# A recurrent attention and a snake MLP in one kernel: v of 13 tiles loaded as float by SyncE, and Strassen's products for two more groups of tiles

## The chip, the cores and the metric

The kernel runs on one core of one Trainium2 chip. A core has five engines, each with its own list of instructions that it takes in order: TensorE (PE in the profile, with its weight loads as PEld), VectorE (DVE), ScalarE (ACT), GpSimd (POOL) and SyncE (SP), which here issues DMAs only. GpSimd issues DMAs too. Instructions of different engines wait for each other by semaphores. The metric is the device time of one execution in microseconds (us), the median over several runs.

## The reference

Per batch and head a decaying state is summed up over 768 tokens, and each token's q reads it. What comes out is an input of an MLP with the function h + sin(alpha h)^2 / alpha. All arrays are float32.

```python
B, H, S, D = 4, 8, 768, 64            # q, k, v: [B, H, S, D]
gamma = 1.0 - 2.0 ** (-5.0 - np.arange(H))
for t in range(S):
    state = gamma[None, :, None, None] * state + np.einsum('bhd,bhe->bhde', k[:, :, t], v[:, :, t])
    y[:, :, t] = np.einsum('bhd,bhde->bhe', q[:, :, t], state) / np.sqrt(D)
x = y.transpose(0, 2, 1, 3).reshape(B * S, H * D)      # [3072, 512]
h = x @ w_in                                           # w_in [512, 2048]
s = np.sin(alpha * h)
out = (h + s * s / (alpha + 1e-09)) @ w_out            # w_out [2048, 512]
```

## The kernel before

The 3072 tokens are 24 tiles of 128 (six per batch). `order`, also called `P`, is the order in which tiles are worked on: P0 to P3 are the first tiles of the four batches, then come the rest of batches 0 and 1 (P4 to P13), and from P14 on batches 2 and 3, in the end alternating. Ten groups follow: g0 with four tiles, g1 to g8 with two each, g9 with four.

**Attention.** A tile's scores, their mask, and the product with v are computed as blocks; what earlier tiles left is read from a state (s_f in float, s_q in bf16). v is scaled by a decay factor (`scale_v`, line 185) before it is used. `burst` (line 458) works on one tile and starts the next one's scores; `pair` (line 537), used for P16 to P21, does two tiles of different batches at once, with one PSUM tile y of two banks. Both write TensorE instructions that need the scaled v of their tiles. q and k are transposed by a DMA that SyncE issues (`turn`, line 294, tile qkT, six buffers) or, for early tiles, by TensorE.

**Loads.** GpSimd issues loads that change float to bf16. For the 11 tiles P0 to P10 a load brings one tile (`load_chunk`); for the 13 others, called wide, `load_seq` (line 131) brings all wide tiles of a batch, with eight DMAs (four heads by two halves of the partitions) for each of q, k and v, into qk_seq and v_seq. Batch 1 has three wide tiles, batches 2 and 3 five each. `scale_v` then works in place, for P9 to P14 on VectorE, for others on GpSimd.

**MLP.** A phase g from 1 to 9 (`phase`, line 878) computes the hidden layer of group g in slots, and beside it the output layer of group g-1. A slot (`Slot`, line 596) takes two of the 16 blocks of 128 hidden columns (in phase 9 one): eight matmuls into a PSUM tile ph, then sine and square on ScalarE (tile s), and the sum on VectorE, which gives gT in bf16 (line 625). The lists `atts` and `behind_slot` say at which slot what else is put, attention's calls, transposes, scales (before the output layer's share of the slot) and mixes (behind it). Each engine runs its instructions in the order in which this program writes them.

The output layer comes in two forms. The plain one (`ff_out`, line 631) has 16 matmuls of 512 columns per tile into a PSUM tile po, a copy by VectorE (line 644) and a store by SyncE. For groups in `fast` (line 653: g8 and g9) a pair of tiles is a product of 2 by 2 blocks (two tiles by two halves of the hidden columns, times two halves by two halves of w_out), done with Strassen's seven products instead of eight: seven times eight matmuls of 256 columns (class `Seven`, line 720). That needs sums and differences of blocks of w_out (`mix_w`, line 675, ten tiles w_mix, each of four blocks) and of gT (`mix_g`, line 687, the sum, difference and cross tiles of g_mix; three instructions for every two of eight block columns). The seven products go to three sums a, b and c in PSUM; a copy of b (`hold`), and adds of a with b (`cross`), of c with b (`rest`) and of a with that (`main`) give the output. Products 4 and 3 read gT itself, products 5 and 2 the sums, 1 the cross tile, 7 and 6 the differences.

PSUM has eight banks: four single ones with the tag mm (ph, po, halves of scores), two for the tag two (y, py, and a with b of g8), two for the tag pa (scores). After phase 9 a last stage (`fast_end`) computes g9's output.

A long string, `PLAN`, gives the order of all work of the start and phase 1; behind it, lines 1046 to 1120 place the rest. GpSimd's list behind PLAN reads: q and k of batch 1, v of P10, v of batch 1, q, k and v of batch 2, q and k of batch 3's first two wide tiles, three scales; then, as `last_loads` at slot (5,5), a weight mix, v of batch 3, two weight mixes, a scale, and the rest of q and k of batch 3.

Of the kernel before, what the change touches and what calls it, by code (L numbers as in the profile page):

```python
# [38 lines left out]
def kernel(  # L39
# [91 lines left out]
    def load_seq(bt, names="qkv", part=slice(None), between=None):  # L131
# [8 lines left out]
        fs = slice(2 * (now[0] - cs[0]), 2 * (now[-1] - cs[0]) + 2)  # L140
        for name, src in (("q", q), ("k", k), ("v", v)):
            if name not in names:
                continue
            for n, (b, m, e) in enumerate(heads):
                if n == 3 and between is not None:
                    scale_v(between, nc.gpsimd)
                r, at = half(b), 2 * m + e
# [1 line left out]
                nc.gpsimd.dma_start(out=o, in_=src[bt, head(b, m, e), now[0] * C:(now[-1] + 1) * C, :].rearrange("(f i) d -> i f d", i=64))  # L149
# [35 lines left out]
    def scale_v(j, eng):  # L185
        t, by = raw["v", j], kg
        if wide(j):
            t, by = t.rearrange("i f p d -> i (f p) d"), kgq
        eng.tensor_mul(t, t, by[:, j % NCH, :, None].to_broadcast([128, H, D]))  # L189
# [474 lines left out]
    w_todo = [(n, i) for n in (4, 3, 1, 7, 6) for i in range(2)]  # L664

    def w_homes():
        for _ in range(5):
            yield big.tile([128, 4, NH], BF16, name="w_mix", tag="qkr", bufs=10)
        for pool, tag, n in ((consts, "dec", 2), (big, "qk_seq1", 3)):
            t = pool.tile([128, n, 4, NH], BF16, name="w_mix", tag=tag)  # L670
            for i in range(n):
                yield t[:, i]
    w_home = w_homes()

    def mix_w(eng):

        n, i = w_todo.pop(0)
# [3 lines left out]
        eng.tensor_tensor(w_mix[n, i], w_block(*a, js), w_block(*b, js), op=op)  # L681
# [465 lines left out]
```

## Time and profile before

| what | value |
|---|---|
| median of three runs | 206.72 us (205.53, 206.93, 206.72) |
| the profiled execution | 207.02 us |
| its span | 205.2 us |
| TensorE busy, granted clock | 195.2 us, 0.997 |
| VectorE, ScalarE, GpSimd busy | 161.5, 151.8, 163.2 us |
| line 610 (ph) and line 634 (po) in the chain that ended last | 37% and 28% of the span |
| GpSimd: loads issued at line 149 | 88 instructions, 59.6 us |
| SyncE's transposes of qk_seq | 13, 6.2 us from issue to landing |

The span is the time from the first to the last instruction in one profiled execution; the time of that execution is a little longer. The chain is followed back from the last instruction, at each step to what released it. In a timeline a row has start, duration, engine, line, operation, output and inputs, and how many instructions were merged; matmuls are pipelined, so a duration of a single one is longer than its distance to the next, and costs are read from start to start.

### The profile page before, as it was taken

The numbers are of one execution on the slowest core, as the hardware profiler recorded it, in microseconds if no ns is written. First come the engines' busy times: TensorE is split into PE (matmuls) and PEld (weight loads), VectorE is DVE, ScalarE is ACT, GpSimd is POOL, SyncE is SP. The second block draws the span as 40 slices with busy tenths as digits, with TensorE's granted clock in tenths as the row PEclk, the third lists the DMA queues.
The fourth block names the chain that finished last, engine by engine and source line by source line (L and its number), as shares of the span: only waits on it lengthen the run. The fifth ranks groups of instructions, "written<-read, shape, count | busy, mean of one in ns | idle before, by whom it ended". The sixth has DMA issues, their size and how long they took to land.

```text
span 205.2 us, 6029 instructions
## 1 busy us (share of the span) xinstructions
PE 195.2 (95%) x2426; PEld 131.4 (64%) x2455; DVE 161.5 (79%) x344; ACT 151.8 (74%) x312; POOL 163.2 (80%) x204
## 2 busy tenths in 40 slices
PE   7889999999998999999999999999999999999993
PEld 7444544557765667666666676666766665555983
DVE  5787499877998887887998885995998775577853
ACT  7678888656996877877877959588586869999120
POOL 8998996999999996997399997999193876997000
PEclk9999999999999999999999999999999999999998
DMA  8999999999999999999996796994406101001123
GB/s 133 147 175 192 201 201 176 167 134 106 231 151 188 104 171 194 170 136 150 143 116 117 89 141 117 120 131 104 105 2 107 51 5 51 3 0 51 54 102 102
DMA packets 103580, 24.82 MB, mean 121 GB/s; under 512 B 93392, under 2 KB 101248, under 8 KB 103552
## 3 DMA queue, kind: packets, MB, share of 16 engines
q0 software_dynamic: 80080, 13.38, 92.8%
q1 hardware_dynamic: 23472, 11.06, 26.8%
q8 instruction: 19, 0.31, 0.7%
q14 instruction: 9, 0.07, 0.1%
HBM read 27.30 MB, written 6.29 MB: 164 GB/s over the span
## 4 chain that ended last, share of the span: by engine, by line
PE 83%; DMA 7%; POOL 4%; issue 2%; DVE 2%; ACT 1%; POOLq 0%
PE ph L610 37%; PE po L634 28%; DMA qkT<-qkr 4%; PE a L756 3%; DMA qkr<-in_q_dram 3%; PE ab L756 3%; POOL qkr L125 2%; PE b L756 2%; PE py L373 1%; POOL vr L125 1%; PE c L756 1%; PE pt L291 1%; PE pa L388 1%; PE py L437 1%; POOL w_in L161 1%
## 5 line engine op out<-in xcount | busy, mean ns | idle before, releaser
L625 DVE SCALAR_TENSOR_TENSOR gT<-s,rec_alpha,ph 128x256 bf16<-128x256 f32 (+3 forms) x164 | 79.4, 522 | 25.1 <-ACT s L618 24.6
L610 PE MATMUL ph<-xT,w_in 128*128 128x256 bf16 (+3 forms) x653 | 98.0, 291 | 0.3
L613 ACT ACTIVATE s<-ph,alpha_sb 128x256 f32<-128x256 f32 (+3 forms) x164 | 75.9, 505 | 28.1 <-PE ph L610 26.3
L610 PEld LDWEIGHTS <-w_in 128*128 128x128 bf16 x656 | 63.1, 98 | 29.6 <-DVE s_f L568 0.7
L634 PE MATMUL po<-w_out,gT 128*128 128x512 bf16 x264 | 70.3, 379 | 2.3 <-issue 1.9
L618 ACT ACTIVATE s<-s 128x512 f32<-128x512 f32 (+1 forms) x94 | 58.7, 626 | 2.8
L634 PEld LDWEIGHTS <-gT 128*128 128x128 bf16 x288 | 26.4, 98 | 20.8 <-DVE gT L625 0.5
L710 POOL TENSOR_TENSOR g_mix<-gT 128x512 bf16<-128x512 bf16 (+1 forms) x27 | 25.9, 994 | 7.2 <-DVE gT L625 7.2
L149 POOL DMA_DIRECT2D qk_seq<-in_q_dram x32 | 21.5, 712 | 6.6 <-DMA v_seq<-in_v_dram 6.1
L149 POOL DMA_DIRECT2D qk_seq<-in_k_dram x32 | 21.3, 720 | 1.5 <-DMA qk_seq<-in_q_dram 1.4
L149 POOL DMA_DIRECT2D v_seq<-in_v_dram x24 | 16.8, 743 | 0.0
L681 POOL TENSOR_TENSOR w_mix<-w_out 128x1024 bf16<-128x1024 bf16 x7 | 15.2, 2190 | 0.0
L756 PEld LDWEIGHTS <-g_mix 128*128 128x128 bf16 x128 | 11.9, 98 | 3.6
L644 DVE COPY o_sb<-po 128x512 f32<-128x512 f32 x15 | 10.3, 687 | 2.0 <-PE po L634 1.6
L125 POOL DMA_DIRECT2D vr<-in_v_dram x11 | 10.3, 932 | 1.2 <-DMA w_in<-in_moe_w_in_dram 0.7
L189 POOL TENSOR_TENSOR v_seq<-v_seq,kgq 128x512 bf16<-128x512 bf16 x9 | 9.8, 1097 | 1.4 <-DMA v_seq<-in_v_dram 1.4
L407 DVE TENSOR_TENSOR aTw<-pa,maskq 128x768 bf16<-128x768 f32 x10 | 9.5, 954 | 0.0
L495 DVE TENSOR_TENSOR xT<-py,qg 128x512 bf16<-128x512 f32 x13 | 8.9, 683 | 0.5 <-PE py L453 0.5
L869 PE MATMUL spare<-warm 128*128 128x112 bf16 (+1 forms) x52 | 7.9, 325 | 1.4 <-DVE warm L199 1.2
L391 DVE TENSOR_TENSOR aT<-pa,mask 128x1024 bf16<-128x1024 f32 x7 | 8.5, 1219 | 0.4 <-PE pa L388 0.4
L520 ACT CAST s_q<-s_f 128x256 bf16<-128x256 f32 x13 | 5.1, 393 | 2.7 <-DVE s_f L515 2.7
L165 POOL DMA_DIRECT2D w_out<-in_moe_w_out_dram x8 | 5.8, 727 | 1.2 <-DMA w_in<-in_moe_w_in_dram 0.8
(138 smaller groups left out, 217.7 us busy)
## 6 DMA issues: line engine op xcount, KB each, us to landing
out_dram<-o_sb SPq DMA_DIRECT2D x21, 256.0 KB, 3.9
w_in<-in_moe_w_in_dram POOLq DMA_DIRECT2D x8, 256.0 KB, 8.3
w_out<-in_moe_w_out_dram POOLq DMA_DIRECT2D x8, 256.0 KB, 7.9
vr<-in_v_dram POOLq DMA_DIRECT2D x11, 128.0 KB, 5.3
v_seq<-in_v_dram POOLq DMA_DIRECT2D x16, 80.0 KB, 4.7
qkr<-in_q_dram POOLq DMA_DIRECT2D x7, 128.0 KB, 6.4
qkr<-in_k_dram POOLq DMA_DIRECT2D x7, 128.0 KB, 5.8
qk_seq<-in_q_dram POOLq DMA_DIRECT2D x16, 48.0 KB, 4.4
```

The lines of the kernel that those rows point to most:

```text
L125: nc.gpsimd.dma_start(out=t, in_=chunk_of(src, j))
L149: nc.gpsimd.dma_start(out=o, in_=src[bt, head(b, m, e), now[0] * C:(now[-1] + 1) * C, :].rearrange("(f i) d -> i f d", i=64))
L189: eng.tensor_mul(t, t, by[:, j % NCH, :, None].to_broadcast([128, H, D]))
L610: nc.tensor.matmul(self.ph[:, m, :], w_in[:, i, f * 128:(f + 1) * 128], xT[g][:, i, self.lo:self.hi], start=(m == 0 and i == 0), stop=(i = ...
L613: nc.scalar.activation(out=self.s[:, m, :], in_=self.ph[:, m, :], func=ACTF.Sin, scale=alpha_sb[:, f:f + 1])
L618: nc.scalar.activation(out=self.s, in_=self.s, func=ACTF.Square)
L625: nc.vector.scalar_tensor_tensor(gT[self.g][:, f, self.lo:self.hi], self.s[:, m, :], rec_alpha[:, f:f + 1], self.ph[:, m, :], op0=ALU.mult ...
L634: nc.tensor.matmul(po[g, ts], gT[g][:, f, ts * C:(ts + 1) * C], w_out[:, f, :], start=(f == 0), stop=(f == FF - 1))
L644: nc.vector.tensor_copy(o_sb, po[g, ts])
L681: eng.tensor_tensor(w_mix[n, i], w_block(*a, js), w_block(*b, js), op=op)
L710: eng.tensor_tensor(o, i0, i1, op=op)
L756: nc.tensor.matmul(t, self.left(n, j), r, start=k not in self.begun, stop=(j == FH - 1), skip_group_check=True)
```

## The change

It has these parts.

1. `fast` gets groups 6 and 7. Their four tiles (two pairs) leave the plain form. Group 6's sums lie in one mm bank (a) and one after the other in the tag two (b, c); group 7's lie in mm banks (a, b, c). `phase` takes a plan that says which products stand in which slot. A pair's two halves of output go out as one DMA; group 8 keeps two.
2. `mix_g` can do sums, differences and cross tiles apart. Group 6's are put at slots (6,1) to (6,7), group 7's at (7,1), (7,3), (7,5), (7,7), all on GpSimd.
3. v of the 13 wide tiles is loaded as float, by SyncE, in five parts (batch 1; batch 2's first three; batch 3's first; batch 2's last two; batch 3's last four), into one tile vf of 16 half tiles, which batch 3 shares with batches 1 and 2. `scale_v` reads vf and writes v_seq. vf takes the buffer of g0's gT, and g9's gT takes it after that.
4. The scales of P10 to P14 go from VectorE to GpSimd; those of P18 to P21 stand later in the list. Weight mixes get other homes (used-up tiles of v, the decay table, and batch 1's q and k), five of ten in halves; eight halves and five whole ones on GpSimd, two halves on VectorE, in place of seven and three whole ones.
5. GpSimd's list and the transposes get another order: behind PLAN come q and k of batch 1 and v of P10, then `loads` at (2,2); the transposes of P12, P17, P18 and P19 stand earlier than before.

```diff
-            for n, (b, m, e) in enumerate(heads):
-                if n == 3 and between is not None:
-                    scale_v(between, nc.gpsimd)
+            if name == "v":
+                vf = raw["vf"][:, 6:16] if bt == 2 else raw["vf"][:, 0:nh]
+                for i, c in enumerate(cs):
+                    raw["vf", bt * NCH + c] = vf[:, 2 * i:2 * i + 2]
+            for n, (b, m, e) in list(enumerate(heads))[some]:
+                if n in between:
+                    between[n]()
...
-                o = tv[r, fs, at, :] if name == "v" else tqk[r, fs, "qk".index(name), at, :]
-                nc.gpsimd.dma_start(out=o, in_=src[bt, head(b, m, e), now[0] * C:(now[-1] + 1) * C, :].rearrange("(f i) d -> i f d", i=64))
+                o = vf[r, fs, at, :] if name == "v" else tqk[r, fs, "qk".index(name), at, :]
+                (nc.sync if name == "v" else nc.gpsimd).dma_start(out=o, in_=src[bt, head(b, m, e), now[0] * C:(now[-1] + 1) * C, :].rearrange("(f i) d -> i f d", i=64))
...
-            t, by = t.rearrange("i f p d -> i (f p) d"), kgq
-        eng.tensor_mul(t, t, by[:, j % NCH, :, None].to_broadcast([128, H, D]))
+            o, t = (x.rearrange("i f p d -> i (f p) d") for x in (t, raw["vf", j]))
+            by = kgq
+        eng.tensor_mul(o, t, by[:, j % NCH, :, None].to_broadcast([128, H, D]))
...
-    fast = (8, 9)
+    fast = (6, 7, 8, 9)
...
+        if g == NG - 3:
+            s = Seven(g, 0, lambda k: psum.tile([128, 2, NH], F32, name=k, tag="mm", bufs=4)[:, slice(0, 2) if k != "c" else 0])
+            parts = [[(4, range(7))], [(4, range(7, FH)), (3, range(6))], [(3, range(6, FH)), (5, range(5))],
+                     [(5, range(5, FH)), (2, range(4))], [(2, range(4, FH)), s.hold], [s.cross, (1, J)], [s.rest, (7, J)],
+                     [(6, J), s.main]]
+            return [s.steps(*p) for p in parts]
+        if g < NG - 3:
...
+            parts = [[(4, J)], [(5, J)], [(2, J), s.hold], [(3, J), s.cross], [(7, range(4))], [(7, range(4, FH)), (6, range(2))],
+                     [(6, range(2, FH)), (1, range(2))], [(1, range(2, FH)), s.rest, s.main]]
+            return [s.steps(*p) for p in parts]
...
-    load_seq(1, "q", between=P[8])
+    load_seq(1, "q", between={3: scaled(P[8])})
     load_seq(1, "k")
     load_chunk(P[10], "v")
-    load_seq(1, "v")
-    load_seq(2, "q")
-    load_seq(2, "k")
-    load_seq(2, "v")
-    load_seq(3, "q", slice(0, 2))
-    load_seq(3, "k", slice(0, 2))
-    for j in P[15:17] + P[18:19]:
-        scale_v(j, nc.gpsimd)
...
-        at(where[n] if n < 16 else (5, 5), X(P[n + 2]))
+        if n != 10:
+            at({15: (4, 6), 16: (4, 5)}.get(n, where[n]), X(P[n + 2]))
...
-    for i, spot in ((19, (6, 2)), (20, (6, 6)), (21, (7, 2)), (22, (7, 6)), (23, (8, 2))):
+    for i, spot in ((18, (6, 6)), (19, (7, 0)), (20, (7, 4)), (21, (7, 6)), (22, (8, 0)), (23, (8, 2))):
         at(spot, lambda j=P[i]: scale_v(j, nc.gpsimd))
...
     def last_loads():
-        mix_w(nc.gpsimd)
-        nc.gpsimd.tensor_copy(seen, st["qkT", P[17]][:, 0, 0:1])
-        load_seq(3, "v")
-        mix_w(nc.gpsimd)
-        mix_w(nc.gpsimd)
+        load_seq(3, "q", slice(2, None))
         scale_v(P[17], nc.gpsimd)
-        load_seq(3, "qk", slice(2, None))
+        load_seq(3, "k", slice(2, None))
...
+    def loads():
+        load_seq(1, "v")
+        turn(P[12])
+        pieces_w(2, "vr")()
+        scale_v(P[10], nc.gpsimd)
+        pieces_w(2, "vr")()
+        load_seq(2, "q")
+        load_seq(2, "k", between={2: scaled(P[11])})
+        scale_v(P[12], nc.gpsimd)
+        scale_v(P[13], nc.gpsimd)
+        load_seq(3, "qk", slice(0, 2))
+
+    at((2, 2), loads)
...
+    for spot, bt, part in (((3, 6), 2, slice(0, 3)), ((4, 6), 3, slice(0, 1)), ((5, 2), 2, slice(3, None)), ((6, 0), 3, slice(1, None))):
+        at(spot, lambda bt=bt, part=part: load_seq(bt, "v", part))
+    for spot in ((4, 0), (4, 2)):
+        mixes(spot, lambda: mix_w(nc.vector, "vr"))
+    for spot, fn in (((3, 6), pieces_w(2, "vr")), ((4, 5), pieces_w(2, "vr")), ((3, 6), pieces_w(1, "dec")), ((3, 6), scaled(P[14], P[15], P[16])),
+                     ((3, 6), pieces_w(1, "dec")), ((4, 5), pieces_w(3, "seq"))):
+        mixes(spot, fn)
+    for spot, m, only in (((6, 1), 0, "s"), ((6, 3), 2, "s"), ((6, 5), 4, "s"), ((6, 5), 0, "dx"), ((6, 6), 2, "d"), ((6, 7), 6, "s"),
+                           ((6, 7), 2, "x"), ((6, 7), 4, "dx"), ((6, 7), 6, "dx")):
+        mixes(spot, lambda m=m, only=only: mix_g(6, m, 2, nc.gpsimd, only))
+    for g in (7, 8):
+        for m in range(0, FH, 2):
+            mixes((g, m + 1), lambda g=g, m=m: mix_g(g, m, 2, nc.gpsimd))
```

More of the change, by code (lines that the diff above doesn't have):

```diff
@@ L129, in wide, with load_seq @@
         return j >= NCH + 3 and j % NCH > 0
-    def load_seq(bt, names="qkv", part=slice(None), between=None):
+    def load_seq(bt, names="qkv", part=slice(None), between={}, some=slice(None)):
         cs = [c for c in range(NCH) if wide(bt * NCH + c)]
@@ L140, in load_seq @@
         fs = slice(2 * (now[0] - cs[0]), 2 * (now[-1] - cs[0]) + 2)
+        if "v" in names and "vf" not in raw:
+            raw["vf"] = work.tile([128, 16, NP, D], F32, name="vf", tag="gA", bufs=1)
         for name, src in (("q", q), ("k", k), ("v", v)):
@@ L663, with mix_w, mix_g @@
              6: ((0, 0), (0, 1), ALU.add), 7: ((1, 0), (1, 1), ALU.add)}
[L664 to L677, printed above, removed]
-        a, b, op = W_MIX[n]
-        js = slice(4 * i, 4 * i + 4)
-        w_mix[n, i] = next(w_home)
-        eng.tensor_tensor(w_mix[n, i], w_block(*a, js), w_block(*b, js), op=op)
+    w_todo = {"vr": [(n, j, 2) for n in (7, 6) for j in range(0, FH, 2)] + [(1, 4, 2), (1, 6, 2)],
+              "dec": [(4, 0, 4), (4, 4, 4)], "seq": [(3, 0, 4), (3, 4, 4), (1, 0, 4)]}
+    w_home = {}
+    def mix_w(eng, home):
+        n, i, c = w_todo[home].pop(0)
+        a, b, op = W_MIX[n]
+        if home == "vr":
+            to = big.tile([128, 2, NH], BF16, name="w_mix", tag="vr", bufs=11)
+        else:
+            if home not in w_home:
+                w_home[home] = (consts if home == "dec" else big).tile(
+                    [128, 2 if home == "dec" else 3, 4, NH], BF16, name="w_mix", tag="dec" if home == "dec" else "qk_seq1")
+            to = w_home[home][:, (2 if home == "dec" else 3) - 1 - len(w_todo[home])]
+        eng.tensor_tensor(to, w_block(*a, slice(i, i + c)), w_block(*b, slice(i, i + c)), op=op)
+        for j in range(c):
+            w_mix[n, i + j] = to[:, j]
     def blocks(t, first, *dims):
         return bass.AP(t.tensor, t.offset + 128 * first, [t.ap[0]] + [[128 * a, n] for a, n in dims if n > 1] + [[1, 128]])
-    def mix_g(g, m, n, eng):
+    def mix_g(g, m, n, eng, only="sdx"):
         w = sizes[g]
-        if m == 0 and w == 2:
+        if m == 0 and "s" in only and w == 2:
             for k in ("s0", "s1", "d0", "d1", "x"):
                 g_mix[g, k] = big.tile([128, 8 * 128], BF16, name="g_mix", tag="qkr", bufs=10)
-        elif m == 0:
+        elif m == 0 and w > 2:
             for k in (2, 3):
@@ L810, in main, with steps @@
                 self.store(1, self.o[:, 1, c], 1, c.start, c.stop)
+        def steps(self, *parts):
+            return [fn for part in parts for fn in ([part] if callable(part) else self.pieces(part))]
         def pieces(self, *parts):
@@ L878, in phase @@
     def phase(g, outs, att, nf=1, on_vector=(), tags={}, early=()):
-        no, done = len(outs), 0
+        plan = outs if outs and isinstance(outs[0], list) else None
+        no, done = 0 if plan else len(outs), 0
         for n in range(FF // nf):
@@ L907, in phase @@
                 run(fresh, "exit", "keep")
+            if g - 1 in fast and n == 5:
+                run(more, "exit1")
             if n + 1 not in early:
@@ L1072, in B, with pieces_w @@
         return lambda: burst(old, new, first, beside=beside, second=second)
+    def pieces_w(n, home):
+        return lambda: [mix_w(nc.gpsimd, home) for _ in range(n)]
     for n in range(9, 17):
@@ L1109 @@
-    for spot in ((7, 0), (7, 2), (7, 6), (7, 7)):
-        mixes(spot, lambda: mix_w(nc.gpsimd))
-    for m in range(0, FH, 2):
-        mixes((8, m + 1), lambda m=m: mix_g(8, m, 2, nc.gpsimd))
+    for spot, bt, part in (((3, 6), 2, slice(0, 3)), ((4, 6), 3, slice(0, 1)), ((5, 2), 2, slice(3, None)), ((6, 0), 3, slice(1, None))):
[5 more added lines that the diff above has]
+        mixes(spot, fn)
```

29 lines of the change are left out of this document (19 added, 10 removed).

## The prediction

> **What bounds the kernel now.** I read the page first (busy shares, then the chain that ended last), then the timelines of TensorE, GpSimd and VectorE from 54 to 170 us, and last the wait list.
>
> ```profile
> span 205.2 us, 6029 instructions
> ...
> PE 83%; DMA 7%; POOL 4%; issue 2%; DVE 2%; ACT 1%; POOLq 0%
> ```
>
> The span is 205.2 us of a profiled execution of 207.02 us, so 1.82 us lie around it; the median of the three runs is 206.72 us, 0.30 us below that execution. TensorE carries 83% of the chain. The stages that the change touches look like this on TensorE (start, duration, line, output and inputs, count):
>
> ```profile
> 109.03 0.31 PE L373 MATMUL py<-qkT,s_q 64*64 64x128 bf16 x8
> ...
> 137.62 1.04 PE L610 MATMUL ph<-xT,w_in 128*128 128x256 bf16 x8
> 138.50 0.81 PE L634 MATMUL po<-w_out,gT 128*128 128x512 bf16 x3
> 139.36 1.04 PE L610 MATMUL ph<-xT,w_in 128*128 128x256 bf16 x8
> ...
> 146.08 0.52 PE L437 MATMUL y<-aTw,v_seq 64*64 64x128 bf16 x32
> ...
> 155.62 0.42 PE L544 MATMUL y<-qkT,s_q 64*64 64x128 bf16 x16
> ...
> 156.17 0.52 PE L437 MATMUL y<-aTw,v_seq 64*64 64x128 bf16 x32
> ...
> 157.50 1.04 PE L610 MATMUL ph<-xT,w_in 128*128 128x256 bf16 x8
> ...
> 169.73 1.03 PE L610 MATMUL ph<-xT,w_in 128*128 128x512 bf16 x4
> ```
>
> I write (g,n) for slot n of phase g. Phase 7 starts at 137.62, with its first eight products ph, slot (8,2) at 157.50, phase 9 at 169.73. A plain slot takes 139.36 - 137.62 = 1.74 us, half ph and half po, with no hole: TensorE is the bound here, and only a shorter list on TensorE, or a new wait of TensorE, moves the end. The pairs of attention tiles stand in (7,4) and (8,1). In each, the 32 products of aTw with v, at 146.08 and 156.17, are the first that need the second tile's scaled v, from the 17th on.
>
> **The change part by part.**
>
> *Strassen's products for groups 6 and 7.* The chain has both kinds of product start to start:
>
> ```profile
> 158.53 0.86 PE po L634 x4
> ...
> 197.70 1.75 PE a L756 x16
> ```
>
> Four po of 512 columns take 0.86 us, 16 products of 256 columns 1.75 us, thus 0.215 and 0.109 us each. A pair of tiles goes from 32 x 0.216 = 6.9 us to 56 x 0.109 = 6.1 us. Two pairs save 1.65 us, all of it on TensorE's path in phases 7 and 8. Up to the start of the pair in (8,1), phase 7 has given 0.83 us and slot (8,0), with 7 products for 4 po, 0.10: together 0.93 us.
>
> ```profile
> 137.62:152.92 15.30, 15.19 (x207) 10.52 (x208) 12.04 (x27) 11.75 (x25) 10.77 (x10) 1.00 0.43 77
> ```
>
> VectorE gets three adds for two copies of po, some 0.7 us more in a phase in which it is busy 12.0 of 15.3 us; ScalarE gets one copy, 0.6 us beside 11.8 of 15.3 us. That slack hides both. In phase 8 the sums a, b and c live in the four one-bank slots, which leaves two banks for ph. A ph lives from its slot's start, 157.50, to the end of its add, 160.98:
>
> ```profile
> 135.02 0.87 DVE L625 SCALAR_TENSOR_TENSOR gT<-s,rec_alpha,ph 128x256 bf16<-128x256 f32 x2
> ...
> 138.50 0.87 DVE L625 SCALAR_TENSOR_TENSOR gT<-s,rec_alpha,ph 128x256 bf16<-128x256 f32 x2
> ...
> 160.11 0.87 DVE L625 SCALAR_TENSOR_TENSOR gT<-s,rec_alpha,ph 128x256 bf16<-128x256 f32 x2 [1.03 <-ACT s L618]
> ```
>
> These are 3.5 us, and two slots now take 3.26, so one slot waits 0.2 us; the other slots have an attention stage between them. I take 0.2, with 0 and 1 as ends.
>
> *GpSimd's list.* Its rows, of two stretches:
>
> ```profile
> 67.28 0.91 POOL L125 DMA_DIRECT2D vr<-in_v_dram  x1 [0.17 <-issue]
> ...
> 73.36 3.85 POOL L149 DMA_DIRECT2D qk_seq<-in_q_dram  x5
> ...
> 102.61 4.28 POOL L149 DMA_DIRECT2D qk_seq<-in_k_dram  x7 [0.51 <-DMA qk_seq<-in_q_dram]
> ...
> 126.06 5.31 POOL L149 DMA_DIRECT2D qk_seq<-in_q_dram  x8
> 131.28 5.35 POOL L149 DMA_DIRECT2D qk_seq<-in_k_dram  x8
> ...
> 148.92 0.61 POOL L577 CAST s_q<-s_f 128x512 bf16<-128x512 f32 x1 [4.54 <-DVE s_f L572]
> 149.49 1.04 POOL L189 TENSOR_TENSOR v_seq<-v_seq,kgq 128x512 bf16<-128x512 bf16 x1
> 150.49 4.21 POOL L681 TENSOR_TENSOR w_mix<-w_out 128x1024 bf16<-128x1024 bf16 x2
> 158.22 2.90 POOL L710 TENSOR_TENSOR g_mix<-gT 128x512 bf16<-128x512 bf16 x3 [3.52 <-DVE gT L625]
> ...
> 171.55 17.17 POOL L710 TENSOR_TENSOR g_mix<-gT 128x512 bf16<-128x512 bf16 x18 [1.57 <-DVE gT L625]
> ```
>
> Start to start: a scale 1.0, the state's cast 0.6, a weight mix of 1024 columns 2.1, three g_mix instructions (sum, difference, cross) 2.86, thus 1.1 + 1.1 + 0.66. A DMA issue costs 0.77 (five in 3.85), 0.61 (seven in 4.28) or 0.66 (eight in 5.31), by its size.
>
> ```profile
> L149 POOL DMA_DIRECT2D v_seq<-in_v_dram x24 | 16.8, 743 | 0.0
> ...
> L253 POOL TENSOR_TENSOR qg<-qg,step 128x512 f32<-128x512 f32 x5 | 5.1, 1044 | 0.1
> ...
> L189 DVE TENSOR_TENSOR v_seq<-v_seq,kgq 128x512 bf16<-128x512 bf16 x4 | 2.7, 684 | 0.0
> ```
>
> GpSimd loses the 24 issues of v, 16.8 us. It gains 24 g_mix instructions (8 x 2.86 = 22.9 us), the scales of P10 to P14 from VectorE (5 x 1.0), and has eight half and five whole weight mixes for seven whole ones (+4.6): some 16 us more in all. A half mix (512 columns) and a scale that reads float have no row. Their nearest are g_mix's sum of the same shape, 1.1, and the decay table's product, float in and out, 1.04; I keep 1.1 and 1.0, with 0.9 and 1.3 as ends.
>
> The new order, from the issue of P10's v, which ends at 68.2: two half mixes to 70.4; P10's scale waits for its data, 5.3 us from issue to landing (next fence), so 73.5, done 74.5; two half mixes 76.7; q and k of batch 2, 16 x 0.77, with three scales between, 92.0; q and k of batch 3, 16 x 0.61, 101.8; two half mixes, a whole one, the scales of P14 to P16, a whole one, 9.4, 111.2; two half and three whole mixes, 8.5, 119.7; the last q, P17's scale, the last k, 11.6, 131.3 us (now 136.6). The sums of g6 for m = 0 and 2 and the state's cast, 2.8, bring it to 134.1. The waits of issues on landings I put at nothing; they are 6.1 and 1.4 us now, and most are for landings of v, which leave this queue. Both ends, 0 and 7.5, stay for the range.
>
> ```profile
> POOL qk_seq L149 <- DMA v_seq<-in_v_dram: 6.1, 4, 2.0
> ...
> POOL qk_seq L149 <- DMA qk_seq<-in_q_dram: 1.4, 4, 0.5
> ```
>
> Next, gT gates: the sum of m = 4 needs the adds of slot (6,5), which end at 135.9 (135.02 + 0.87), that of m = 6 those of (6,7), 139.4. From 135.9: sum m4 1.1, difference and cross m0 1.76, P18's scale 1.0, difference m2 1.1, sum m6 1.1 (142.0), cross m2 0.66, difference and cross of m4 and m6 3.5, P19's scale 1.0, together 11.2, so 147.1. Then two triples of g7 5.7, P20's scale 1.0, the cast 0.6, a triple 2.86, P21's scale 1.0, together 11.2: **158.3 us**, with no hole in the list.
>
> Who waits for that: slot (7,1) needs the sum m6 from 140.9 on and gets it at 142.0; the pair in (7,4) wants P19 at 146.3 and gets it at 147.1; the pair in (8,1) wants P21 half way through the products of 156.17, so at 156.4 - 0.93 = 155.5. These waits don't add up, since a wait at (7,1) moves the later needs along; the last decides: 158.3 - 155.5 = 2.8 us on TensorE. Behind it all is in time: P22's scale at 162.2 for a burst at 164, g8's last sum at 172.8 for a use after 176, g9's fifth triple at 188.9 for an end stage that starts at 191.
>
> *v as float by SyncE.* The parts stand in SyncE's queue between the transposes and the stores. Behind the first part is P12's transpose, behind P14's transpose the second part, and with it the scale of P14: done by the list above at 101.8 + 2.2 + 2.1 + 1.0 = 107.1, used in the burst at 109.03. The other dues are wider. With some 2 us to spare I put this part at nothing, as long as landings take today's 5 us or so. VectorE loses five scales of 0.68 us; it wasn't the bound, so nothing comes of that.
>
> ```profile
> q0 software_dynamic: 80080, 13.38, 92.8%
> q1 hardware_dynamic: 23472, 11.06, 26.8%
> ...
> vr<-in_v_dram POOLq DMA_DIRECT2D x11, 128.0 KB, 5.3
> ```
>
> *A rule that speaks against it.* The packets of the two queues took 92.8% and 26.8% of 16 engines' span, together more than the span: the queues' packets overlap. The Trainium skill, DMA: Bandwidth & Descriptors, section Issuing engines are not separate DMA queues, says that DMAs of all issuers run on the same 16 engines, and that spreading them saves only the time to issue. By that rule the issues' waits would stay, and the sum would be that of rival (3), 213 us, instead of 208; no run here has shown v on the other queue.
>
> *Sum.* -1.65 (products) + 2.8 (P21's wait) + 0.2 (banks) = +1.3 us; phase 9 and the end stage keep their time. 206.72 + 1.3 = **208.0 us** against the median (208.3 against the profiled execution).
>
> **The rivals.**
>
> (1) GpSimd is in time: 206.72 - 1.65 = 205.1 us. If its list from 135.9 to P21 took 19.6 us instead of 22.4 (13% less), only the saving would stay. For it: just two adds gate this list, so any shorter instruction shortens it. Against it: 17.17 us for 18 g_mix hold the mean at 0.95 us with no wait inside, and a scale was 1.04.
>
> (2) The loads or SyncE's queue are late: 210 to 211 us. P14's path (k's landing, transpose, scale, burst) has some 2 us to spare, and GpSimd has 1.8 us until 135.9; beyond that each us is a wait of TensorE. Late by 4 to 5 us gives 2 to 3 us on 208.0. For it: the second part of v waits in the queue behind a transpose that waits for k. Against it: k of batch 2 is issued by 92, as late as now within 5 us, and 17 us before the burst.
>
> (3) The issues' waits stay: 213 us. With 7.5 us more GpSimd is at 134.1 + 7.5 = 141.6 less the 0.5 that the cast waits for its state, so 141.1 instead of 135.9: 5.2 us on 208.0. Against it: most of these waits name v, and the q and k that remain go out with mixes and scales between them.
>
> (4) The products don't pay, 206.7 + 2.8: 56 weight loads for 32 in each pair. Against it: the end stage's 16 products in 1.75 us have a load each already.
>
> **How the numbers follow.** A measurement of this kernel can tell about 1%, 2.1 us, from no change. The forecast has 0.55; 5% of the 22.4 us list is 1.1 us, so its own range is 206.9 to 209.1, of which 0.42 lies within 1% and 0.13 above it. GpSimd in time has 0.20: 0.12 within 1%, 0.08 beyond, since 1.65 us lies only 0.4 us short of that bound and the three runs differ by more (205.53 to 206.93). Late loads: 0.15, of it 0.14 above 1%. Waits stay: 0.08, above. Products that don't pay: 0.02, within or at the bound. So faster 0.08, same 0.57, slower 0.35. The range leaves out the outer tail of (1) and the upper parts of (2) and (3): 204.9 to 210.6 us.
>
> **What would show it.** In the changed profile: 112 products of 256 columns for 64 po in phases 7 and 8; GpSimd without a hole from 136 to 158 us; TensorE's waits in phases 7 and 8 named after GpSimd's scale of v_seq or its g_mix; GpSimd's waits on landings near 1 us. The forecast is wrong if P21's scale ends before TensorE asks for it, if TensorE waits for a transpose or a landing between 62 and 122 us, or if the issues' waits stay above 6 us.

## The result, and the profile after

The changed kernel takes 208.55 us (median of 20 runs) beside 206.55 us for the kernel before on the same chip (20 runs): a ratio of 1.0105, with a 95% interval from 1.0076 to 1.0133. That is 0.55 us above the forecast and inside the range. The prediction took 1% as what can be told from no change; the ratio lies just past that bound and its interval has the bound inside. So the change costs about 1%, on the border between the "same" to which it gave 0.57 and the "slower" to which it gave 0.35.

The profiled execution took 208.07 us. Its page shows a GpSimd that now stands in the chain that ended last with 19%, where it had 4%, and queues whose load is spread anew:

```profile
span 206.3 us, 6203 instructions
...
q0 software_dynamic: 66384, 11.67, 74.1%
q1 hardware_dynamic: 37936, 14.47, 37.8%
...
PE 61%; POOL 19%; DMA 8%; DVE 5%; issue 3%; ACT 3%; POOLq 0%; ACTq 0%
```

The line numbers of the changed kernel are higher: ph is L617, po L641, Strassen's products L765, g_mix L719, the scale L197, the load L155, the add that makes gT L632. TensorE's timeline (the same columns as before) shows where its list now has holes:

```profile
136.89 1.04 PE L617 MATMUL ph<-xT,w_in 128*128 128x256 bf16 x8
137.76 1.21 PE L765 MATMUL a<-w_mix,gT 128*128 128x256 bf16 x8
...
141.41 0.39 PE L765 MATMUL b<-w_out,g_mix 128*128 128x256 bf16 x2 [0.91 <-POOL g_mix L719]
...
148.25 1.05 PE L617 MATMUL ph<-xT,w_in 128*128 128x256 bf16 x8 [0.17 <-DVE s_f L575]
...
157.63 0.32 PE L428 MATMUL pa<-v_seq,qk_seq 64*64 64x64 bf16 x16 [1.08 <-POOL v_seq L197]
...
170.89 1.03 PE L617 MATMUL ph<-xT,w_in 128*128 128x512 bf16 x3
```

Phase 7 starts at 136.89 and phase 9 at 170.89: phases 7 and 8 take 34.00 us, where they took 169.73 - 137.62 = 32.11. The difference, 1.89 us, is nearly all of the 2.00 us between the medians. (The two profiled executions are only 1.05 us apart, since the changed one reached phase 7 sooner by 0.73 us; at 62.30 the kernel before had waited 1.14 us for a transposed tile, a wait that some of the traces here have and others not.) TensorE waits twice for GpSimd, 0.91 us in slot (7,1) for a sum of g6 and 1.08 us in the pair at (8,1) for P21's scale. GpSimd's timeline over the same stretch has no hole from 135.24 on:

```profile
126.33 5.37 POOL L155 DMA_DIRECT2D qk_seq<-in_k_dram  x8
131.59 2.40 POOL L719 TENSOR_TENSOR g_mix<-gT 128x512 bf16<-128x512 bf16 x2
133.80 0.73 POOL L584 CAST s_q<-s_f 128x512 bf16<-128x512 f32 x1
135.24 2.89 POOL L719 TENSOR_TENSOR g_mix<-gT 128x512 bf16<-128x512 bf16 x3 [0.71 <-DVE gT L632]
138.09 1.04 POOL L197 TENSOR_TENSOR v_seq<-vf,kgq 128x512 bf16<-128x512 f32 x1
139.09 6.37 POOL L719 TENSOR_TENSOR g_mix<-gT 128x512 bf16<-128x512 bf16 x7
145.41 1.05 POOL L197 TENSOR_TENSOR v_seq<-vf,kgq 128x512 bf16<-128x512 f32 x1
...
156.53 1.05 POOL L197 TENSOR_TENSOR v_seq<-vf,kgq 128x512 bf16<-128x512 f32 x1
```

The last row is P21's scale. It ends at 157.58, and TensorE's instruction that waited for it starts at 157.63.

A table of the two phases serves all that follows. The starts are those of the first ph of phases 7, 8 and 9 in each kernel's TensorE timeline; the ratio is to the kernel before on the same chip.

| kernel | starts | phase 7 | phase 8 | both | ratio (95%) |
|---|---|---|---|---|---|
| before | 137.62, 152.92, 169.73 | 15.30 | 16.81 | 32.11 | 1 |
| changed | 136.89, 153.31, 170.89 | 16.42 | 17.58 | 34.00 | 1.0105 (1.0076 to 1.0133) |
| GpSimd's order | 136.66, 152.09, 168.40 | 15.43 | 16.31 | 31.74 | 0.9987 (0.9960 to 1.0013) |
| loads alone | 137.69, 152.99, 169.80 | 15.30 | 16.81 | 32.11 | 1.0005 (0.9978 to 1.0033) |
| scales on VectorE | 136.89, 154.46, 170.83 | 17.57 | 16.37 | 33.94 | 1.0089 (1.0058 to 1.0120) |
| the same, other slots | 137.74, 153.17, 170.22 | 15.43 | 17.05 | 32.48 | 1.0025 (0.9994 to 1.0056) |
| products dealt out anew | 145.40, 160.56, 177.13 | 15.16 | 16.57 | 31.73 | 1.0021 (0.9990 to 1.0052) |
| group 7 alone | 135.88, 151.17, 167.43 | 15.29 | 16.26 | 31.55 | 0.9982 (0.9949 to 1.0015) |
| group 6 alone | 137.07, 152.51, 169.31 | 15.44 | 16.80 | 32.24 | 1.0025 (0.9994 to 1.0056) |

The ratios leave out disturbed executions (of the 40 above 217.14 and 218.59 us before, 210.28 and 701.96 us changed), and the profile of the kernel with products dealt out anew is of such a one (214.32 us), with a granted clock of 1.00 in the two phases, so that only what lies in these is read from it.

### The profile page after: what moved, and what is told of

Same layout as the page of the kernel before. It is cut to its first block, busy times and chain, and to the rows that moved or that the text cites. A ratio compares the mean times of both kernels' runs of the same rounds, so it can differ in the third digit from the quotient of the medians.

```text
span 206.3 us, 6203 instructions
## 1 busy us (share of the span) xinstructions
PE 194.3 (94%) x2479; PEld 135.4 (66%) x2503; DVE 159.0 (77%) x340; ACT 152.9 (74%) x314; POOL 178.7 (87%) x214
## 4 chain that ended last, share of the span: by engine, by line
PE 61%; POOL 19%; DMA 8%; DVE 5%; issue 3%; ACT 3%; POOLq 0%; ACTq 0%
PE ph L617 27%; PE po L641 17%; POOL g_mix L719 8%; POOL qk_seq L155 5%; DMA qkT<-qkr 5%; PE a L765 4%; PE ab L765 3%; DMA qkr<-in_k_dram 2%; POOL v_seq L197 2%; PE b L765 2%; DVE gT L632 1%; PE py L380 1%; ACT s L620 1%; PE c L765 1%; POOL qkr L125 1%
## 5 line engine op out<-in xcount | busy, mean ns | idle before, releaser
L632 DVE SCALAR_TENSOR_TENSOR gT<-s,rec_alpha,ph 128x256 bf16<-128x256 f32 (+3 forms) x164 | 79.6, 522 | 26.9 <-ACT s L625 25.2
L617 PE MATMUL ph<-xT,w_in 128*128 128x256 bf16 (+3 forms) x652 | 98.1, 290 | 0.5 <-DVE s_f L575 0.2
L617 PEld LDWEIGHTS <-w_in 128*128 128x128 bf16 x656 | 63.1, 98 | 26.8 <-DVE s_f L575 0.7
L641 PE MATMUL po<-w_out,gT 128*128 128x512 bf16 x206 | 54.8, 379 | 1.9 <-issue 1.6
L719 POOL TENSOR_TENSOR g_mix<-gT 128x512 bf16<-128x512 bf16 (+1 forms) x51 | 49.1, 1006 | 2.4 <-DVE gT L632 2.0
L641 PEld LDWEIGHTS <-gT 128*128 128x128 bf16 x224 | 20.5, 98 | 16.5 <-DVE gT L632 0.5
L155 POOL DMA_DIRECT2D qk_seq<-in_k_dram x32 | 21.5, 744 | 2.8 <-DMA qk_seq<-in_q_dram 2.8
L155 POOL DMA_DIRECT2D qk_seq<-in_q_dram x32 | 21.4, 713 | 2.5 <-DMA qkr<-in_k_dram 1.9
L765 PEld LDWEIGHTS <-g_mix 128*128 128x128 bf16 x208 | 19.4, 98 | 6.2 <-POOL g_mix L719 1.2
L686 POOL TENSOR_TENSOR w_mix<-w_out 128x512 bf16<-128x512 bf16 (+1 forms) x13 | 19.8, 1630 | 0.0
L197 POOL TENSOR_TENSOR v_seq<-vf,kgq 128x512 bf16<-128x512 f32 x13 | 13.8, 1096 | 0.0
L765 PEld LDWEIGHTS <-gT 128*128 128x128 bf16 x88 | 7.9, 98 | 2.2 <-DVE gT L632 0.3
L765 PE MATMUL b<-w_out,g_mix 128*128 128x256 bf16 x64 | 8.5, 273 | 0.9 <-POOL g_mix L719 0.9
L651 DVE COPY o_sb<-po 128x512 f32<-128x512 f32 x11 | 7.6, 690 | 1.8 <-PE po L641 1.4
L765 PE MATMUL a<-w_mix,gT 128*128 128x256 bf16 (+1 forms) x72 | 8.7, 261 | 0.0
L897 PE MATMUL spare<-warm 128*128 128x112 bf16 (+1 forms) x52 | 7.0, 297 | 1.4 <-DVE warm L207 1.2
```

The costliest lines, as they stand in the source:

```text
L155: (nc.sync if name == "v" else nc.gpsimd).dma_start(out=o, in_=src[bt, head(b, m, e), now[0] * C:(now[-1] + 1) * C, :].rearrange("(f i) d ...
L197: eng.tensor_mul(o, t, by[:, j % NCH, :, None].to_broadcast([128, H, D]))
L617: nc.tensor.matmul(self.ph[:, m, :], w_in[:, i, f * 128:(f + 1) * 128], xT[g][:, i, self.lo:self.hi], start=(m == 0 and i == 0), stop=(i = ...
L632: nc.vector.scalar_tensor_tensor(gT[self.g][:, f, self.lo:self.hi], self.s[:, m, :], rec_alpha[:, f:f + 1], self.ph[:, m, :], op0=ALU.mult ...
L641: nc.tensor.matmul(po[g, ts], gT[g][:, f, ts * C:(ts + 1) * C], w_out[:, f, :], start=(f == 0), stop=(f == FF - 1))
L686: eng.tensor_tensor(to, w_block(*a, slice(i, i + c)), w_block(*b, slice(i, i + c)), op=op)
```

## The experiments

### Is it GpSimd's order?

Only the place of four instructions in GpSimd's list is changed: the scales of P18 to P21 stand among the mixes of g6, behind the sums that slot (7,1) needs and ahead of the triples of g7. Nothing is added or removed.

```diff
-    for i, spot in ((18, (6, 6)), (19, (7, 0)), (20, (7, 4)), (21, (7, 6)), (22, (8, 0)), (23, (8, 2))):
+    for i, spot in ((22, (8, 0)), (23, (8, 2))):
...
-                           ((6, 7), 2, "x"), ((6, 7), 4, "dx"), ((6, 7), 6, "dx")):
+    mixes((6, 7), scaled(P[18], P[19]))
+    for m, only in ((2, "x"), (4, "dx"), (6, "dx")):
+        mixes((6, 7), lambda m=m, only=only: mix_g(6, m, 2, nc.gpsimd, only))
+    mixes((6, 7), scaled(P[20], P[21]))
```

> Same instructions as the changed kernel; only GpSimd's order differs: the sum m6 of group 6 stands ahead of P18's scale, then P18 and P19, and P20 and P21 stand right behind group 6's mixes, ahead of those of group 7. Theory 1 (GpSimd's list decides when TensorE gets on in phases 7 and 8): the waits of TensorE for g_mix in (7,1) (0.9 us) and for the scale of v_seq in (8,1) (1.1 us) go, and nothing else gets late, so 2.0 to 2.8 us less than the changed kernel: ratio to the kernel before 0.996 to 1.001. Rival 1 (the time went into the Strassen phases themselves: PSUM banks, VectorE, ScalarE): less than 0.7 us is won, ratio 1.007 or more.

It took 206.00 us, 0.9987 of the kernel before. GpSimd's timeline has the scales in pairs, P20's and P21's done by 148.24 instead of 157.58:

```profile
135.01 5.12 POOL L719 TENSOR_TENSOR g_mix<-gT 128x512 bf16<-128x512 bf16 x5 [1.73 <-DVE gT L632]
140.09 2.04 POOL L197 TENSOR_TENSOR v_seq<-vf,kgq 128x512 bf16<-128x512 f32 x2
142.09 4.15 POOL L719 TENSOR_TENSOR g_mix<-gT 128x256 bf16<-128x256 bf16 x5
146.20 2.04 POOL L197 TENSOR_TENSOR v_seq<-vf,kgq 128x512 bf16<-128x512 f32 x2
148.20 5.75 POOL L719 TENSOR_TENSOR g_mix<-gT 128x512 bf16<-128x512 bf16 x6
```

TensorE's two waits for GpSimd are gone, and phases 7 and 8 take 31.74 us, 2.26 us less than in the changed kernel. So GpSimd's order alone makes the loss over the kernel before. But the products save 1.65 us, and 32.11 - 1.65 would be 30.46: the remaining 1.28 us are other holes of TensorE. Its timeline shows where, and the rows of its weight loads (PEld) with a wait show for what:

```profile
136.66 1.04 PE L617 MATMUL ph<-xT,w_in 128*128 128x256 bf16 x8
137.53 1.21 PE L765 MATMUL a<-w_mix,gT 128*128 128x256 bf16 x8
138.58 1.04 PE L617 MATMUL ph<-xT,w_in 128*128 128x256 bf16 x8
...
146.25 0.61 PE L765 MATMUL a<-w_mix,g_mix 128*128 128x256 bf16 x4
147.03 1.05 PE L617 MATMUL ph<-xT,w_in 128*128 128x256 bf16 x8 [0.17 <-DVE s_f L575]
...
159.03 0.93 PE L765 MATMUL b<-w_out,g_mix 128*128 128x256 bf16 x7
160.06 1.03 PE L617 MATMUL ph<-xT,w_in 128*128 128x256 bf16 x8
```

```profile
138.45 0.10 PEld L765 LDWEIGHTS <-gT 128*128 128x128 bf16 x1 [0.28 <-DVE gT L632]
...
140.18 0.11 PEld L765 LDWEIGHTS <-g_mix 128*128 128x128 bf16 x2 [0.20 <-POOL g_mix L719]
...
147.03 0.77 PEld L617 LDWEIGHTS <-w_in 128*128 128x128 bf16 x8 [0.45 <-DVE s_f L575]
...
150.33 0.11 PEld L765 LDWEIGHTS <-g_mix 128*128 128x128 bf16 x2 [0.35 <-DVE xT L568]
```

Eight products should take 8 x 0.109 = 0.87 us; from 137.53 to the next ph they take 1.05. Four from 146.25 should end 0.44 us later; the next ph starts 0.78 later, because its bank, pa, is not free until the pair's state add is done. Seven from 159.03 should take 0.76 and take 1.03. Taken slot by slot against the kernel before (a plain slot's length, less 0.86 us for four po, plus 0.109 for each product), phase 7 has 0.95 us of such holes: 0.18 in (7,0), 0.09 in (7,1), 0.40 in (7,4), 0.26 in (7,6); and phase 8 has 0.33, of which 0.27 in (8,3).

The rows name the causes in phase 7. In (7,0) the eighth product takes the last block of gT, which the add of slot (6,7) has just made. In (7,1) the last two wait for GpSimd's sum m6, the one hole that GpSimd still has a part in. Behind (7,4) ph waits for the state add, and in (7,6) sum c waits for the exits of y (line 568), whose two banks it takes over. In (8,3) VectorE's timeline settles it: the next ph, at 160.06, needs the bank of a ph whose add ends at 160.00:

```profile
159.13 0.87 DVE L632 SCALAR_TENSOR_TENSOR gT<-s,rec_alpha,ph 128x256 bf16<-128x256 f32 x2 [0.90 <-ACT s L625]
```

### Do the loads cost anything?

The new loads, v as float by SyncE and the new order stay; groups 6 and 7 have their plain products, and the loop that places group 6's mixes is gone with group 7's.

```diff
-    fast = (6, 7, 8, 9)
+    fast = (8, 9)
...
-    for g in (7, 8):
+    for g in (8,):
         for m in range(0, FH, 2):
```

> The changed kernel with Strassen's products only for groups 8 and 9, as before, and without the mixes of gT for groups 6 and 7; v as float by SyncE, the order of loads and the weight mixes stay. Theory 1: the loads' part costs and brings nothing, so the time of the kernel before, ratio 0.997 to 1.003, with GpSimd's idle time back in phases 6 and 7. Rival 2 (the queue of SyncE or the sharing of the DMA engines costs part of the 2 us): ratio 1.004 or more, with a wait of TensorE between 62 and 122 us.

It took 206.48 us, 1.0005 of before, and its phases 7 and 8 have the lengths of the kernel before to the hundredth. GpSimd's timeline there has its idle time back:

```profile
148.99 0.61 POOL L584 CAST s_q<-s_f 128x512 bf16<-128x512 f32 x1 [8.95 <-DVE s_f L579]
149.56 2.04 POOL L197 TENSOR_TENSOR v_seq<-vf,kgq 128x512 bf16<-128x512 f32 x2
158.29 2.89 POOL L719 TENSOR_TENSOR g_mix<-gT 128x512 bf16<-128x512 bf16 x3 [6.69 <-DVE gT L632]
```

The loads by SyncE are free, and they alone bring nothing.

### Why v had to leave GpSimd

v goes back to GpSimd, cast on the way and scaled in place, in the same five parts at the same places of the program.

```diff
-                o = vf[r, fs, at, :] if name == "v" else tqk[r, fs, "qk".index(name), at, :]
-                (nc.sync if name == "v" else nc.gpsimd).dma_start(out=o, in_=src[bt, head(b, m, e), now[0] * C:(now[-1] + 1) * C, :].rearrange("(f i) d -> i f d", i=64))
+                o = tv[r, fs, at, :] if name == "v" else tqk[r, fs, "qk".index(name), at, :]
+                nc.gpsimd.dma_start(out=o, in_=src[bt, head(b, m, e), now[0] * C:(now[-1] + 1) * C, :].rearrange("(f i) d -> i f d", i=64))
...
-            o, t = (x.rearrange("i f p d -> i (f p) d") for x in (t, raw["vf", j]))
+            o, t = (x.rearrange("i f p d -> i (f p) d") for x in (t, t))
```

> The changed kernel with v of the 13 tiles loaded by GpSimd again, cast to bf16 on the way, in the same parts and at the same places of the program, and scaled in place. Theory 1 (GpSimd has no idle time between 68 and 158 us, so what its queue gets is added): 40 issues of 0.65 us put some 26 us on its list, TensorE waits for the state's cast, the mixes and the scales, and the time is 225 to 235 us. Rival (GpSimd's waits on landings take up the issues): up to 7 us of them go into time it waited anyway, and the time is below 220 us.

One run took 232.91 us. Its groups by line have the issues at 0.65 us each, within the prices taken from the kernel before, and its wait list has TensorE behind GpSimd:

```profile
L155 POOL DMA_DIRECT2D v_seq<-in_v_dram x40 | 26.1, 765 | 1.0 <-DMA qk_seq<-in_k_dram 0.9 <-issue 0.2
```

```profile
PE b L765 <- POOL g_mix L719: 6.9, 4, 4.3
...
PE pa L428 <- POOL v_seq L197: 6.2, 2, 4.2
```

So a full list passes on nearly all that is put on it: 26.1 us of issues cost 24.4 us beside the changed kernel's median, and P21's scale ends at 182.36, 24.8 us later than in the changed kernel. Its waits on landings hide almost none of it. TensorE's waits for GpSimd make 17.9 us of that (the two rows, and 4.8 us for a scale in the pairs); behind such waits its granted clock fell too, to 0.51 from 160 to 170 us.

### Could VectorE do the scales?

The scales of P18 to P21 stay at their slots and go to VectorE.

```diff
-        at(spot, lambda j=P[i]: scale_v(j, nc.gpsimd))
+        at(spot, lambda j=P[i]: scale_v(j, nc.vector if j in P[18:22] else nc.gpsimd))
```

> The changed kernel with the scales of P18 to P21 on VectorE in place of GpSimd, at the same slots. Theory 1: GpSimd's list is 1 us shorter ahead of the sum m6 and 4 us shorter ahead of g7's last mix; both waits of TensorE go, ratio to the kernel before 0.996 to 1.001. If VectorE, with 2.7 us more in phases 6 and 7, holds up adds of gT, up to 1 us of that is lost. Rival 1: ratio 1.007 or more.

This missed: 208.03 us, 1.0089 of before. The wait for P21's scale is gone, but phase 7 takes 17.57 us. VectorE's timeline, and the rows of TensorE's with a wait over 0.4 us, show the new one:

```profile
146.82 1.32 DVE L197 TENSOR_TENSOR v_seq<-vf,kgq 128x512 bf16<-128x512 f32 x1
148.06 0.95 DVE L414 TENSOR_TENSOR aTw<-pa,maskq 128x768 bf16<-128x768 f32 x1
148.93 0.41 DVE L575 TENSOR_TENSOR s_f<-s_f,pa 128x256 f32<-128x256 f32 x1
...
153.34 0.68 DVE L197 TENSOR_TENSOR v_seq<-vf,kgq 128x512 bf16<-128x512 f32 x1
```

```profile
139.17 0.28 PE L765 MATMUL a<-w_mix,gT 128*128 128x256 bf16 x1 [0.46 <-DVE gT L632]
...
149.39 1.05 PE L617 MATMUL ph<-xT,w_in 128*128 128x256 bf16 x8 [1.40 <-DVE s_f L575]
```

P20's scale, written at (7,4), stands on VectorE ahead of the mask and the state add of the same slot, and these free bank pa for the next ph. The wait that was 0.17 us is 1.40 (the 1.05 in the next expectation is the length of the ph row, misread). To see whether the place or VectorE's load is at fault, the same four scales, still on VectorE, were put at slots without the first pair:

```diff
-    for i, spot in ((18, (6, 6)), (19, (7, 0)), (20, (7, 4)), (21, (7, 6)), (22, (8, 0)), (23, (8, 2))):
+    for i, spot in ((18, (7, 1)), (19, (7, 2)), (20, (7, 7)), (21, (8, 0)), (22, (8, 0)), (23, (8, 2))):
```

> The scales of P18 to P21 on VectorE as in the earlier run on VectorE (208.03 us, 1.0089 of before), but at slots (7,1), (7,2), (7,7) and (8,0), none of them beside the first pair. Theory 1 (that run lost its gain because P20's scale of 1.3 us stood ahead of the mask and the state's add that free bank pa): the wait of ph for the state's add falls from 1.05 us to 0.2 to 0.4 us, phases 7 and 8 take 31.8 to 32.5 us, and the time is 0.997 to 1.003 of before. Rival (VectorE has no room for the scales beside GpSimd's mixes anywhere in phase 7): the add of gT comes late elsewhere, TensorE waits for it, and the time stays at 1.005 to 1.010.

It took 206.66 us, 1.0025 of before; phase 7 is 15.43 us, as with GpSimd's order, and the wait for the state add is 0.17 us again. Phase 8 has one new wait, of 0.62 us, at 155.59 for an add of VectorE (`main`). The places were at fault, P20's above all; at the new ones VectorE's load costs the 0.74 us by which phase 8 is longer than with GpSimd's order (17.05 beside 16.31).

### What more GpSimd work costs

P20's scale is done three times on GpSimd at (7,4), and in a second kernel twice; the repeats write the same values.

```diff
+    for _ in range(2):
+        at((7, 4), lambda: scale_v(P[20], nc.gpsimd))
```

> The changed kernel with P20's scale done three times on GpSimd at (7,4): two instructions of 1.0 us more, with the same result. Theory 1: GpSimd's list has no slack before P21's scale, so the time grows by the full 2.0 us: ratio to the kernel before 1.019 to 1.022, and TensorE's wait in (8,1) grows from 1.1 to 3.1 us. Rival 1: growth under 0.7 us, ratio under 1.015.

It took 211.66 us, 1.0266 (1.0222 to 1.0309), and in the profile its phases 7 and 8 take 37.81 us, 3.81 more than in the changed kernel for the 2.1 us that were added. TensorE's wait for P21's scale is 3.25 us, 2.17 more than in the changed kernel, as it should be. What is more comes behind the wait. In a table by stretches the columns behind the five engines are the granted clock, the DMA share and GB/s:

```profile
157.20:161.00 3.80, 0.55 (x52) 0.52 (x47) 0.43 (x2) 0.96 (x2) 3.80 (x5) 1.00 0.45 89
161.00:164.40 3.40, 3.40 (x31) 2.42 (x19) 2.52 (x5) 0.00 (x0) 3.40 (x5) 0.52 0.00 0
164.40:166.00 1.60, 1.60 (x16) 1.39 (x15) 0.00 (x0) 1.47 (x4) 1.60 (x2) 0.96 0.00 0
```

For 3.4 us the granted clock is 0.52, though TensorE is busy all the time. Whether a shorter wait does this too was asked with the second kernel:

> P20's scale is done twice on GpSimd at (7,4), one more than in the changed kernel, one fewer than in the run with three. Each theory has TensorE wait about 2.1 to 2.2 us in the second pair for P21's scale, 1.0 to 1.1 us more than in the changed kernel. Theory 1 (the run with three lost 1.6 us beyond its wait because TensorE stood still for 3.25 us, and the clock fell only after that): the granted clock of the 6 us behind the wait stays at 1.00 and phases 7 and 8 take 35.0 to 35.2 us. Rival (any wait of some 2 us brings the clock down): the granted clock falls below 0.9 behind it and the two phases take 35.8 us or more.

The rival was right, by one run (210.39 us). The wait is 2.19 us, and the clock falls behind it as before:

```profile
159.60:163.20 3.60, 3.60 (x21) 2.65 (x19) 1.97 (x5) 1.37 (x4) 3.60 (x4) 0.55 0.00 0
163.20:166.00 2.80, 2.80 (x36) 2.29 (x37) 1.65 (x4) 1.93 (x6) 2.80 (x4) 0.97 0.03 6
```

Its phases 7 and 8 take 16.44 and 20.10 us. Against the 16.31 of the kernel with GpSimd's order that is 3.79 us for a wait of 2.19. In the changed kernel a wait of 1.08 us cost 17.58 - 16.31 = 1.27 us, and the clock stayed at 1.00. Whether every execution loses its clock so is open: the four runs with three scales lie between 211.18 and 212.47 us and have mean clocks from 0.981 to 1.0, and the lower clock does not go with the longer time throughout.

### Where the saving of the products goes

Two of the three larger holes of phase 7 are taken away, on top of GpSimd's order: seven products instead of eight in (7,0), whose eighth needs the add of slot (6,7), and all of sum c in (7,7), so that none waits for the exits of y.

```diff
-            parts = [[(4, J)], [(5, J)], [(2, J), s.hold], [(3, J), s.cross], [(7, range(4))], [(7, range(4, FH)), (6, range(2))],
-                     [(6, range(2, FH)), (1, range(2))], [(1, range(2, FH)), s.rest, s.main]]
+            parts = [[(4, range(7))], [(4, range(7, FH)), (5, range(7))], [(5, range(7, FH)), (2, J), s.hold], [(3, J), s.cross],
+                     [(7, range(4))], [(7, range(4, FH)), (6, range(2))], [(6, range(2, FH))], [(1, J), s.rest, s.main]]
```

> GpSimd's order as in the kernel with the scales placed among the mixes (206.0 us, 0.9987 of before), and the products of group 6 dealt out anew: seven instead of eight in slot (7,0), so that none waits for the add of slot (6,7), and the eight of sum c all in (7,7), so that none waits for the exits of y. Theory 1 (the holes of 0.18 us at 137.53 and 0.26 us at 150.34 are waits of TensorE that add up): phases 7 and 8 take 31.3 us instead of 31.74 and the time is 0.995 to 0.998 of before. Rival (VectorE, busy from 144 to 152 us without a gap, sets the pace there, so that a hole closed at one place opens at the next): 31.6 to 31.8 us and 0.998 to 1.000. The wait for the state's add in the slot behind the first pair (0.3 us) stays under both.

It took 206.54 us, 1.0021 (0.9990 to 1.0052), which is not theory 1. In the profile phase 7 falls from 15.43 to 15.16 us, and phase 8 rises from 16.31 to 16.57. The hole in (7,6) is gone. That in (7,0) has only moved on: (7,1) now has 0.28 us instead of 0.09, because a weight load there waits for GpSimd's sum m6, which needs the same add of slot (6,7):

```profile
148.93 0.10 PEld L765 LDWEIGHTS <-g_mix 128*128 128x128 bf16 x1 [0.38 <-POOL g_mix L719]
```

In phase 8 the slots with attention, (8,1), (8,4) and (8,6), are longer by 0.10, 0.16 and 0.09 us, and one without is shorter by 0.09. Whether VectorE's pace is behind that, as the rival has it, stays open.

The last two kernels have the products for one group alone, and no mixes of the other: group 7 with the changed kernel's order of scales, group 6 with the scales among its mixes (`fast` is (6, 8, 9)).

```diff
-    fast = (6, 7, 8, 9)
+    fast = (7, 8, 9)
```

> The changed kernel with Strassen's products for group 7 alone; group 6 has its plain products po again and no mixes of g6. Slot by slot, the kernel with the scales placed among the mixes has holes of 0.95 us against the plain slots in phase 7 and 0.33 us in phase 8, for a saving of 0.83 us in each. Theory 1 (the holes belong to each group's own sums): phase 7 takes 15.3 us, phase 8 16.3 us, together 31.6 us after 32.11 in the kernel before, with no wait for GpSimd, and the time is 0.995 to 1.000 of before. Rival (VectorE and ScalarE can't follow more than they do, so holes open wherever time is saved): the two phases take 31.9 to 32.1 us and the time is 0.999 to 1.003.

> Strassen's products for group 6 alone, the scales of P18 to P21 on GpSimd among the mixes of g6; group 7 has plain products. Theory 1 (the holes of phase 7, 0.95 us, are worth as much as the 0.83 us that its products save): phase 7 takes 15.3 to 15.5 us after 15.30, phase 8 16.8 us as before, together 32.1 to 32.3 us, and the time is 0.998 to 1.003 of before. Rival (the saving of group 6 is real, and the holes come from the two groups' load on VectorE and ScalarE together): phase 7 takes 14.6 to 15.0 us and the two phases 31.4 to 31.8 us.

Both came out as theory 1 has it. Group 7's products alone bring phase 8 from 16.81 to 16.26 us, with no wait for GpSimd; group 6's alone leave phase 7 at 15.44, where the plain products took 15.30. The holes of phase 7 are all there with nothing of group 7 about.

Group 7 alone has the lowest ratio measured, 0.9982 (205.80 us), but its interval (0.9949 to 1.0015) does not set it apart from the kernel before.

## Why the prediction was right, point by point

**The mechanism held.** The sum was -1.65 + 2.8 + 0.2 = +1.35 us over phases 7 and 8, and they took 1.89 us more. Taken apart by the kernel with GpSimd's order: -1.65 for the products (1.62 by the prediction's own rounded factors), +1.28 for the other holes, and 34.00 - 31.74 = +2.26 for GpSimd's lateness. The products' own price was right: with GpSimd's order eight of them start at 143.03 and the next ph follows at 143.91, 0.88 us later, and there are 56 in each pair.

**GpSimd's list was right to within 0.7 us over 90 us, in part by luck.** Its last issue of k ends at 131.70 (131.3 in the forecast), P19's scale at 146.46 (147.1) and P21's at 157.58 (158.3). Counted from the start of phase 7, P21's scale ends after 20.69 us, and the forecast had 158.3 - 137.62 = 20.68. The luck is ahead of 131.70: 3.2 us of waits for landings had been put at nothing, but P10's scale waited 0.4 us for its data instead of the forecast's 3.1. A scale that reads float cost 1.04 and 1.05 us; half mixes of w_out, without a row before, 2.38 us for two at 69.31 and 2.27 at 73.09.

**The term that was mis-sized is "I take 0.2, with 0 and 1 as ends", for the banks.** It is 1.28 us, beyond the upper end. The working looked at phase 8, where it found one slot that waits 0.2 us; that slot is (8,3), with 0.27, and of its cause and size the prediction was right. Phase 7 was put at nothing, and it has 0.95 us, of two kinds. One is a wait that was always near and that po had covered: in the kernel before, the pair's state add ended at 147.60, and ph followed at 147.71.

```profile
147.19 0.41 DVE L568 TENSOR_TENSOR s_f<-s_f,pa 128x256 f32<-128x256 f32 x1
```

With four products in place of four po, TensorE is there 0.40 us too soon. The others are needs that the plain po did not have, 0.53 us in all: product 4 takes the last block of gT in the first slot already, where po takes its blocks in order and comes to the last one in (7,3), product 5 takes the mixes at once, and sum c needs a bank of y. With that, "phase 7 has given 0.83 us" by the pair in (8,1) was wrong as well: it gave nothing.

**P21's wait is therefore shorter than 2.8.** TensorE, late by its own holes, comes to the pair later, so GpSimd is less late. The need also comes a little earlier than was read: the first instructions that want P21's v are not the products of aTw but the state sums ahead of them, the row at 157.63. In all it is 2.26 us, in two pieces, as "a wait at (7,1) moves the later needs along" has it: 0.91 in (7,1), 1.08 in (8,1), and 0.1 to 0.2 us to get going again at each. The pair in (7,4) did not wait, since (7,1) had moved it. The two errors, +1.08 and -0.54, make the 0.54 us by which the sum was short; that they have opposite signs, and that the time came out so near the forecast, is partly luck.

**SyncE's part cost nothing**, as put: the kernel with the loads alone is at 1.0005, and TensorE waits for no landing between 62 and 122 us that it did not wait for before. The claim "GpSimd's waits on landings near 1 us" was too good. The waits for landings of v went, but those for q remain:

```profile
POOL qk_seq L155 <- DMA qk_seq<-in_q_dram: 2.8, 3, 1.6
...
POOL qk_seq L155 <- DMA qkr<-in_k_dram: 0.4, 1, 0.4
```

That is 3.2 us for the 7.5 of before, both from 62 us on; another 1.5 us, for a landing of k, lie just ahead, at 60.89, where the kernel before had none. They cost TensorE nothing, since GpSimd still had to wait 0.71 us for the add that gates its list at 135.24.

**The rivals.** (1), GpSimd in time, did not happen in this kernel, but its price was tested: in time, TensorE does not gain 1.65 us but 0.37. (2), late loads, is excluded by the loads alone. (3), waits of issues that stay, fell: with the one at 60.89 the waits are 4.7 us for 7.5, and GpSimd was in time for its gate. The Trainium skill, DMA: Bandwidth & Descriptors, section Issuing engines are not separate DMA queues, grants a spread over issuers only the time to issue, and that is what the run with v back on GpSimd shows to matter: 26.1 us of it. (4) fell in its mechanism, since 56 weight loads for 32 cost nothing in slots without a hole; but the products do pay little, 0.37 of 1.65 us, because of the holes, and group 6's pay nothing.

## What to carry to other kernels

An instruction that is taken off the bounding engine saves its time only where what follows is ready. Before counting the saving, list for each slot what the new instructions need (a block, a sum, a bank) and when that is ready, and what the old, longer ones had covered. On an engine whose list has no holes, the order decides who waits; the places of four short instructions among long ones gave back 2.26 us here, more than the change's own saving. When a short instruction moves to another engine, look at what stands behind it in that queue, above all at what frees a bank.
